# A 32-pair attention kernel with soft mixture of experts: row-tiled score products, block-diagonal queries, one fp32 memory product, padded v, and a new order of all attention operations

## The chip, the cores and the metric

The kernel runs on one core of one Trainium2 chip. The metric is the device time of one execution in microseconds; the time given for a kernel is the median of its runs. The engines named below are PE (matrix products; PEld is its loading of the stationary operand), DVE (vector), ACT (scalar, activations), POOL (GpSimd) and SP, whose queue issues nearly all DMAs.

## The reference

```
scores = scale * q @ k.T, causal mask, softmax over keys        # B 8, H 8, S 576, D 64
local  = a @ v
q_p    = where(q > 0, q, exp(q) - 1) + 1
mem    = (q_p @ M_prev) / (q_p @ z_prev + 1e-6)
x      = g * mem + (1 - g) * local          # g = sigmoid(beta) per head; x: 4608 x 512
# soft mixture of experts on x: 32 slots (8 experts x 4)
logits = x @ phi; dispatch = softmax over tokens; combine = softmax over slots
slot_out = relu((dispatch.T @ x) @ w1) @ w2                     # w1, w2: 33.5 MB
out    = combine @ slot_out
```

All data are fp32. The scores are spread widely enough (q and k are scaled by 8) that they are formed from parts: each operand is split into a high part that the fast one-pass format fp32r holds, and the low rest.

## The kernel before

**Pairs.** The attention goes over 32 pairs of heads, numbered n; a pair's two heads lie on partitions 0-63 and 64-127 of q. A pair's score rows are cut into tiles: `q1h0 ... q3h1` are 128 query rows of one head, with 256, 384 and 512 keys; `a`, `b` and `z` hold 64 query rows of both heads (rows 0-63, 64-127 and 512-575), and `zb` is the last 64 keys of `z`.

**Scores before.** `X` holds q's high part on the head's own 64 rows and the low part on the other head's rows, so a product with contraction over all 128 rows gives (high + low) times k. `K2` and `KL` hold k's high and low part, on both heads' rows; therefore k comes from memory with both heads on all 128 rows. A tile of one head takes two products of 128 rows (L485 with `K2`, L486 with `KL`). `z` takes four such products (L477 to L480) against zeros in `X`; `a`, `b` and `zb` are plain fp32 products of 64x64 tiles (L474), one for each head. The parts are made by `qhi`, `qlo`, `kn`, `kl`, one operation for each head, on the engine that a table `EV` names (helpers: L399 copies on ACT, L402 on DVE, L404 on POOL; subtractions L453 for q, L459 for k).

**The rest of a pair.** DVE adds the mask and takes each row's maximum (`max`, L514), ACT the exponential (`exp`, L522), PE transposes the result in six banks (`t`, L613), ACT or DVE copies these to `at` (`te`), PE multiplies by v (`av` and `memb`, L673) into PSUM. phi(q) (`qmin`, `qexp`, `qphi`) gives the norms (`norm`, L571), which go through DRAM to be spread over rows (`nrw`, `nrr`: DMA rd, then rb) and scale phi(q) (`qn`, L603); the softmax sums go the same way (`rec`, L527 to L529; `rt`, `rte`, `rrw`, `rrr`: DMA rs, then rm). The memory's product `mema` uses a high and low part of M (`mh`, `ml`) and of phi(q) (`qh`, `ql`) in three fp32r products (L666 to L668) and one fp32 product for 64 rows (L669). `mo` and `xe` add up x on DVE.

**Blocks and the end.** Whenever 512 of the 4608 tokens are complete over the four pairs of a batch, this block is taken into the slots' sums (`x1` ... `x5`). After the last pair the experts' two layers run (L1020, L1037), and the outputs are combined and written (L1094, L1096). 46 of 64 weight tiles of 512 KB are loaded by `w` operations before the experts start; 18 are loaded while they run.

**Order.** A string `SEQ` lists every attention operation; each engine issues its instructions in that order, and waits on semaphores for what the others make. PSUM: two slots of two banks for scores (psS), three banks for everything else (psT), one for `av` (psO). `X`, `K2`, `KL`, `at` and v have one buffer each, k and the exponentials two.

Of the kernel before, what the change touches and what calls it, by code (L numbers as in the profile page):

```python
# [46 lines left out]
qhi.0@0 qhi.1@0 qmin@0 qlo.1@0 qlo.0@0 kn.0@0 gate@0 loadm@0 qexp@0 loadq@1 kl.0@0 w@0 kn.1@0 qphi@0 loadm@1 s.zb@0:0
s.a@0 kl.1@0 s.b@0 loadk@1 s.q3h0@0:1 loadq@2 max.a@0 max.b@0 s.q3h1@0 exp.a@0 max.zb@0 loadk@2 mh@0 exp.b@0 norm@0:0
ml@0 max.q3h0@0 loadv@0 s.q2h0@0 neps@0 s.q2h1@0 qmin@1 nmk@0 exp.q3h0@0 max.q3h1@0 qexp@1 max.q2h0@0 s.q1h1@0:1 s.z@0
exp.q3h1@0 max.q2h1@0 w@1 nred@0 exp.q2h1@0 s.q1h0@0 qphi@1 qhi.1@1 nrw@0 exp.q2h0@0 s.b@1:0 max.z@0 qlo.1@1 norm@1:1  # L50
kn.0@1 t.2@0:2 max.q1h0@0 kn.1@1 kl.0@1 s.a@1 t.1@0:0 exp.q1h0@0 max.b@1 te.2@0 qhi.0@1 s.zb@1 kl.1@1 exp.b@1 qlo.0@1
# [5 lines left out]
te.1@1 s.q2h0@2 qn@1 s.q1h0@2:0 loadv@1 te.0@1 s.q1h1@2 s.q2h1@2 rec@1 loadk@4 t.3@1:2 w@4 t.2@1:0 te.3@1 w@5 s.z@2
te.2@1 mo@0 rt@1:2 mema@0:0 rte@1 rrw@1 t.5@1:2 max.q1h0@2 mh@1 xe.0@0 ml@1 te.5@1 max.q2h1@2 t.4@1:1 exp.q1h0@2 xe.1@0
exp.q2h1@2 qh@1 loadm@2 te.4@1 x3.0@0:2 ql@1 qmin@2 x3e.0@0 memb@1:0 max.a@2 av.0@1 max.zb@2 max.z@2 qexp@2 exp.a@2
av.3@1 qphi@2 exp.z@2 av.2@1 max.q2h0@2 loadq@4 av.1@1 max.q1h1@2 exp.q2h0@2 max.b@2 rrr@1 av.6@1 exp.q1h1@2 norm@2:1  # L60
t.5@2:2 exp.b@2 neps@2 s.q3h1@2:0 loadv@2 te.5@2 nmk@2 mema@1:1 max.q3h1@2 kn.1@3 qhi.1@3 nred@2 t.3@2:2 kl.1@3
exp.q3h1@2 loadm@3 s.q3h0@2 qmin@3 nrw@2 te.3@2 s.zb@3:1 mo@1 s.b@3 qlo.1@3 s.a@3 kn.0@3 qhi.0@3 qexp@3 max.zb@3 max.b@3
max.q3h0@2 exp.b@3 qlo.0@3 s.q2h1@3 nrr@2 qphi@3 exp.q3h0@2 s.q3h1@3:0 max.q2h1@3 mh@2 norm@3:2 kl.0@3 rec@2 loadq@5
exp.q2h1@3 xe.0@1 neps@3 max.a@3 nmk@3 rt@2:2 ml@2 exp.a@3 t.1@2:0 nred@3 loadk@5 rte@2 s.q3h0@3 xe.1@1 te.1@2 nrw@3
t.4@2:2 rrw@2 qn@2 t.2@2:0 te.4@2 x3.1@0:1 qh@2 te.2@2 s.q2h0@3 x3e.1@0 memb@2:2 max.q2h0@3 t.0@2:0 max.q3h0@3
exp.q2h0@3 s.q1h0@3:1 s.q1h1@3 nrr@3 ql@2 s.z@3 exp.q3h0@3 max.q3h1@3 te.0@2 mema@2:1 kn.0@4 max.q1h0@3 rrr@2 exp.q3h1@3
max.z@3 kl.0@4 s.b@4:0 s.a@4 qmin@4 av.0@2 qhi.0@4 max.a@4 loadm@4 qexp@4 max.b@4 max.q1h1@3 qlo.0@4 t.2@3:0 qn@3
exp.z@3 av.2@2 qphi@4 exp.q1h1@3 av.1@2 exp.q1h0@3 xe.0@2 s.zb@4 mh@3 exp.a@4 av.3@2 ml@3 rec@3 kn.1@4 norm@4:2 av.6@2
exp.b@4 max.zb@4 neps@4 kl.1@4 s.q3h0@4:1 loadv@3 te.2@3 mo@2 t.4@3:2 qhi.1@4 max.q3h0@4 t.1@3:0 te.4@3 s.q2h0@4 loadk@6
qlo.1@4 te.1@3 exp.q3h0@4 rt@3:2 nmk@4 t.0@3:0 max.q2h0@4 rte@3 rrw@3 nred@4 s.q3h1@4 te.0@3 s.q2h1@4 xe.1@2 exp.q2h0@4  # L70
t.5@3:2 max.q2h1@4 memb@3:0 t.3@3:1 te.5@3 max.q3h1@4 s.z@4:0 exp.q2h1@4 nrw@4 loadq@6 te.3@3 s.q1h1@4 s.q1h0@4 qh@3
qhi.1@5 s.b@5:1 qhi.0@5 av.0@3 max.q1h1@4 kn.1@5 rrr@3 max.q1h0@4 ql@3 exp.q1h1@4 max.z@4 av.1@3 exp.q1h0@4 qlo.1@5
nrr@4 exp.z@4 kl.1@5 av.3@3 t.3@4:2 exp.q3h1@4 mema@3:1 qlo.0@5 kn.0@5 rec@4 s.zb@5 loadm@5 s.a@5 qmin@5 av.2@3 xe.0@3
kl.0@5 max.zb@5 qexp@5 av.6@3 max.a@5 t.1@4:0 max.b@5 loadv@4 mo@3 exp.a@5 s.q3h1@5:0 te.3@4 mh@4 s.q2h1@5 xe.1@3
loadk@7 ml@4 s.q3h0@5 exp.b@5 max.q2h1@5 rt@4:2 x1.0@0:1 rte@4 max.q3h0@5 exp.q2h1@5 rrw@4 te.1@4 x1.1@0 exp.q3h0@5
t.2@4:2 qn@4 t.4@4:0 x1l@0 te.2@4 s.q2h0@5 x1m@0 te.4@4 t.0@4:1 max.q2h0@5 t.5@4:2 x1e@0 qphi@5 memb@4:0 exp.q2h0@5 qh@4
s.q1h0@5:1 s.z@5 te.5@4 loadq@7 te.0@4 rrr@4 ql@4 s.q1h1@5 kn.0@6 qhi.0@6 av.0@4 max.q1h1@5 kn.1@6 max.q1h0@5 exp.q1h1@5
norm@5:2 x1d@0 max.z@5 qlo.0@6 exp.q1h0@5 av.1@4 neps@5 max.q3h1@5 exp.z@5 x2@0:1 nmk@5 mema@4:2 kl.0@6 qhi.1@6
exp.q3h1@5 x2m@0 s.a@6:1 loadm@6 av.3@4 mh@5 max.a@6 ml@5 x2e@0 rec@5 av.2@4 exp.a@6 qmin@6 nred@5 av.6@4 s.zb@6 loadv@5
s.b@6 x2a@0 mo@4 s.q3h0@6:0 nrw@5 rt@5:1 s.q2h0@6 max.q3h0@6 qlo.1@6 qexp@6 rte@5 exp.q3h0@6 xe.1@4 rrw@5 t.2@5:1 qphi@6  # L80
te.2@5 x4.0@0:2 xe.0@4 norm@6:1 x4a.0@0 t.1@5:0 neps@6 x2s@0 nrr@5 x3.3@0:2 te.1@5 x3.2@0:1 x3e.3@0 nmk@6 t.0@5:0 nred@6
loadq@8 x3e.2@0 t.3@5:2 max.q2h0@6 nrw@6 te.0@5 x4.1@0:1 max.zb@6 max.b@6 rrr@5 te.3@5 kl.1@6 t.5@5:0 exp.b@6 x4a.1@0
x5@0:2 exp.q2h0@6 s.q3h1@6 qn@5 loadk@8 t.4@5:1 x5e@0 max.q3h1@6 s.q2h1@6 nrr@6 qh@5 x3.0@1:2 te.4@5 exp.q3h1@6
s.q1h1@6:0 ql@5 s.q1h0@6 s.z@6 te.5@5 x3e.0@1 max.q2h1@6 memb@5:1 av.0@5 kn.0@7 kn.1@7 max.q1h1@6 max.q1h0@6 exp.q1h1@6
qhi.0@7 kl.0@7 av.3@5 exp.q1h0@6 qlo.0@7 av.2@5 max.z@6 exp.q2h1@6 t.3@6:2 qn@6 exp.z@6 qhi.1@7 av.1@5 kl.1@7 qlo.1@7
av.6@5 s.a@7:1 rec@6 loadv@6 s.zb@7 te.3@6 t.1@6:0 mo@5 s.q3h0@7:0 te.1@6 rt@6:2 s.q3h1@7 rte@6 mema@5:0 rrw@6
# [1108 lines left out]
```

## Time and profile before

| | before |
|---|---|
| runs | 549.18, 553.72, 554.17 us; median 553.72 us |
| profiled execution | span 551.3 us from its first to its last instruction; the page gives no time beside the span |
| PE / DVE / ACT / POOL busy | 494.6 / 446.1 / 374.4 / 269.9 us |
| attention, first to last `rec` | 20.5 to 457.3 us: 31 steps of 14.09 us |
| DMA | 104.94 MB, mean 190 GB/s |

Busy is the time in which an engine has an instruction under way. PE's matrix products are pipelined, and the end of each is modelled, so PE's busy time also holds the tails of products. The chain is the path of work and waits that ended last, followed back from the last instruction.

### The profile page before, as it was taken

Reading aid. Unit: us, or ns where it says so; the run is one execution under the profiler, and the core shown is the slowest. Engines: PE = TensorE matmul, PEld = TensorE weight load, DVE = VectorE, ACT = ScalarE, POOL = GpSimd, SP = SyncE. Lnnn points to the kernel's source line nnn. Section 1 sums busy time; section 2 is a strip of 40 time slices with the busy share of each in tenths; the row PEclk is TensorE's granted clock in tenths of the full one; section 3 lists DMA queues with packets and bytes.
Section 4 is the critical chain, followed back from the end, with each engine's and each line's share of the span. In section 5 each row is a group of like instructions: output and inputs, shape, how many; then the busy total and the mean of one; then the engine's idle time right before and its main releaser. Section 6 shows DMA issues by size and latency. Waiting matters only on the chain.

```text
span 551.3 us, 12391 instructions
## 1 busy us (share of the span) xinstructions
PE 494.6 (90%) x4002; PEld 318.8 (58%) x4002; DVE 446.1 (81%) x1422; ACT 374.4 (68%) x1048; POOL 269.9 (49%) x328
## 2 busy tenths in 40 slices
...
GB/s 302 143 277 142 116 139 118 116 254 182 99 241 215 110 181 140 98 276 114 173 116 183 183 152 127 171 105 154 375 139 147 138 101 299 356 260 413 103 335 321
DMA packets 65776, 104.94 MB, mean 190 GB/s; under 512 B 10736, under 2 KB 41008, under 8 KB 65712
## 3 DMA queue, kind: packets, MB, share of 16 engines
...
q8 instruction: 32, 0.52, 0.4%
q14 instruction: 32, 0.26, 0.2%
q10 hardware_dynamic: 288, 0.09, 0.1%
...
## 4 chain that ended last, share of the span: by engine, by line
DVE 32%; PE 32%; DMA 17%; ACT 6%; issue 5%; POOL 2%; SPq 2%; DVEq 0%; ACTq 0%; POOLq 0%
DMA rb<-rd 8%; PE psT L613 6%; DVE q L514 5%; DVE zq L514 4%; PE oa L673 3%; DMA rd<-rq 3%; PE pf L1020 3%; PE psS L485 3%; DVE KL L459 3%; PE pc L1094 2%; PE psS L486 2%; DMA w<-in_w_dram 2%; DVE qp L603 2%; DVE rq L587 2%; DVE rn L583 2%
## 5 line engine op out<-in xcount | busy, mean ns | idle before, releaser
L522 ACT ACTIVATE q<-q,nm 128x512 f32<-128x512 f32 (+2 forms) x160 | 97.9, 613 | 38.7 <-DVE nm L514 36.8
L399 ACT COPY at<-psT 128x512 f32<-128x512 f32 (+1 forms) x230 | 101.2, 484 | 30.7 <-PE psT L613 18.5
L673 PE MATMUL oa<-at,mv 128*64 128x192 f32 (+4 forms) x640 | 103.0, 437 | 0.0
L485 PE MATMUL psS<-K,X 128*128 128x512 f32 (+2 forms) x192 | 77.4, 410 | 16.3 <-DVE nm L514 14.0
L522 ACT ACTIVATE zq<-zq,nm 128x256 f32<-128x256 f32 (+2 forms) x128 | 69.0, 540 | 24.7 <-DVE nm L514 24.0
L453 POOL TENSOR_TENSOR X<-qq,X 64x64 fp32r<-64x64 f32 (+2 forms) x89 | 81.6, 929 | 8.2 <-DVE X L402 2.4
L613 PE MATMUL psT<-cs,q 128*128 128x128 f32 x480 | 78.3, 285 | 6.4 <-DVE xt L716 2.6
L514 DVE CUSTOM_DVE_ANT_0 q<-psS,mv 128x512 f32<-128x512 f32 (+1 forms) x128 | 76.6, 613 | 3.6 <-PE psS L486 2.4
L613 PEld LDWEIGHTS psT<-cs,q 128*128 128x128 f32 x480 | 56.3, 144 | 19.9 <-DVE xt L716 5.6
L486 PE MATMUL psS<-KL,X 128*128 128x512 f32 (+2 forms) x192 | 65.5, 349 | 1.5 <-DVE KL L459 1.0
L673 PEld LDWEIGHTS oa<-at,mv 128*64 128x64 f32 (+1 forms) x640 | 36.9, 135 | 49.4 <-issue 37.0
L404 POOL TENSOR_SCALAR K<-k 128x512 fp32r<-128x512 f32 x28 | 17.9, 640 | 82.1 <-PE psS L479 56.3
L485 PEld LDWEIGHTS psS<-K,X 128*128 128x128 f32 x192 | 37.4, 195 | 26.7 <-DVE nm L514 15.1
L613 PE MATMUL psT<-cs,zq 128*128 128x128 f32 x288 | 49.7, 283 | 1.0 <-ACT at L399 0.7
L558 POOL TENSOR_SCALAR qp<-qq 128x576 f32<-128x576 f32 x24 | 39.7, 1653 | 19.6 <-PE psT L534 9.2
L459 DVE TENSOR_TENSOR KL<-k,K 128x512 fp32r<-128x512 f32 x50 | 46.6, 933 | 0.2
L603 DVE TENSOR_TENSOR qp<-qp,rb 128x576 f32<-128x576 f32 x32 | 27.6, 863 | 20.3 <-DMA rb<-rd 20.3
L404 POOL TENSOR_SCALAR X<-qq 64x384 fp32r<-64x384 f32 (+2 forms) x75 | 34.3, 471 | 17.2 <-issue 6.9
L486 PEld LDWEIGHTS psS<-KL,X 128*128 128x128 f32 x192 | 37.9, 197 | 3.2 <-DVE KL L459 1.6
L613 PEld LDWEIGHTS psT<-cs,zq 128*128 128x128 f32 x288 | 32.2, 141 | 12.6 <-issue 3.4
L660 POOL TENSOR_TENSOR zq<-qp,zq 128x512 fp32r<-128x512 f32 x26 | 34.7, 1336 | 9.1 <-ACT zq L399 7.5
L522 ACT ACTIVATION_READ_ACCUMULATOR q<-q,nm 128x1 f32 x160 | 30.6, 191 | 0.0
...
## 6 DMA issues: line engine op xcount, KB each, us to landing
...
```

The lines of the kernel that those rows point to most:

```text
L399: nc.scalar.copy(o, i)
L404: ENG = dict(a=act, v=dve, p=lambda o, i: nc.gpsimd.tensor_scalar(out=o, in0=i, scalar1=1.0, scalar2=1.0, op0=ALU.mult, op1=ALU.mult))
L453: ALU_ENG[ev(f"qlo.{h}", n)].tensor_tensor(out=x[ROW[1 - h]], in0=i, in1=x[ROW[h]].bitcast(F32), op=ALU.subtract)
L459: ALU_ENG[ev(f"kl.{h}", n)].tensor_tensor(out=KL[:, h, :], in0=st[n]["k"][h][:, 0:512], in1=K2[:, h, :].bitcast(F32), op=ALU.subtract)
L485: nc.tensor.matmul(o, x[:, h, c:c + 128], k2[:, h, 0:N], start=True, stop=False)
L486: nc.tensor.matmul(o, x[:, h, c:c + 128], kl[:, h, 0:N], start=False, stop=True)
L514: nc.vector.tensor_tensor_reduce(out=sm, in0=src, in1=msk, op0=ALU.add, op1=ALU.min, scale=-0.125, scalar=m0, accum_out=acc_o)
L522: nc.scalar.activation(sm, sm, AF.Exp, scale=-1.0, bias=s["nm"][:, J:J + 1], accum_out=s["sum"][:, J:J + 1])
L558: ALU_ENG[ev("qmin", n)].tensor_scalar(out=st[n]["qp"], in0=st[n]["q"], scalar1=0.0, scalar2=None, op0=ALU.min)
L603: nc.vector.tensor_tensor(out=s["qp"], in0=s["qp"], in1=s["rb"], op=ALU.mult)
L613: nc.tensor.transpose(out=ps[:, 128 * x:128 * x + 128], in_=src[:, k0:k0 + 128], identity=ident)
L673: nc.tensor.matmul(o[ROW[h], col:col + nx], vt[rows, c, ROW[h]], st[n]["at"][rows, a0 + hs * h:a0 + hs * h + nx], start=start, stop=stop)
```

## The change

1. **Row-tiled scores** (`op_s`, new L433). `X` holds q's high part in one plane and its low part in the other, each head on its own 64 rows; `K2` the same for k. Three products per head, each over 64 rows, give high x high + low x high + high x low; the two heads' products alternate and write to different PSUM banks, for which `z` moves between `q1h0` and `q1h1`.
2. **Block-diagonal queries** (L427). q comes with 384 more columns: for `a`, `b` and `z` a 128x128 block that holds head 0's 64 rows and head 1's 64 rows on its diagonal. These tiles become one fp32 product over 128 rows for both heads; `z` is cut at a bank's end into two of 256 keys.
3. **One split per pair.** `qhi`, `qlo`, `kn`, `kl` run once per pair on 128 partitions (128x384 for q, 128x512 for k) instead of once per head; k comes once (288 KB instead of 576 KB a pair), q with its blocks (480 KB instead of 288 KB).
4. **The memory in one fp32 pass** (L592): `mh`, `ml`, `qh`, `ql` go; one fp32 product of 512 columns.
5. **Padded v.** v has six chunks, with zeros in the unused halves of the first and last, so that `av` and `memb` always contract over 128 rows; it is loaded in two DMAs.
6. **Smaller edits.** `rec` takes two DVE instructions instead of three; `at` is one fixed tile; 44 instead of 46 weight tiles are loaded before the experts.
7. **New order.** `SEQ`, `EV` and `WORD` (where weight tiles go) are written anew.

```
 def op_s(n, t):
...
-        if t in ("a", "b", "zb"):
-            for h in range(2):
-                r = ROW[h]
-                lo, k0, k1, c = {...}[t]
-                nc.tensor.matmul(ps[r, c:c + k1 - k0], s["q"][r, lo:lo + 64], s["k"][h][r, k0:k1], start=True, stop=True)
-        elif t == "z":
...
-        else:
-            i, h = int(t[1]), int(t[3])
-            c = 128 * (i - 1) + 128 * h
-            o = ps[:, c0:c0 + N]
-            nc.tensor.matmul(o, x[:, h, c:c + 128], k2[:, h, 0:N], start=True, stop=False)
-            nc.tensor.matmul(o, x[:, h, c:c + 128], kl[:, h, 0:N], start=False, stop=True)
+        if t in ("a", "b", "z", "zb"):
+            i, k0, k1, c = {...}[t]
+            cuts = [k0] + [x - c + k0 for x in (512,) if c < x < c + k1 - k0] + [k1]
+            for x0, x1 in zip(cuts, cuts[1:]):
+                nc.tensor.matmul(ps[:, c + x0 - k0:c + x1 - k0], s["qd"][:, i], s["k"][:, x0:x1], start=True, stop=True)
+        else:
+            i = int(t[1])
+            for x, y in ((0, 0), (1, 0), (0, 1)):
+                for h in range(2):
+                    c0, N = WHERE[f"{t}h{h}"][1:3]
+                    nc.tensor.matmul(ps[:, c0:c0 + N], X[ROW[h], x, 128 * i - 128:128 * i], K2[ROW[h], y, 0:N],
+                                     start=(x, y) == (0, 0), stop=(x, y) == (0, 1))
...
-    [("q1h0", 0, 256), ("q1h1", 256, 256), ("z", 512, 576)],
+    [("q1h0", 0, 256), ("z", 256, 576), ("q1h1", 768, 256)],
...
-    def op_kl(n, h):
-        ALU_ENG[ev(f"kl.{h}", n)].tensor_tensor(out=KL[:, h, :], in0=st[n]["k"][h][:, 0:512], in1=K2[:, h, :].bitcast(F32), op=ALU.subtract)
+    def op_kl(n):
+        ALU_ENG[ev("kl", n)].tensor_tensor(out=K2[:, 1, :], in0=st[n]["k"][:, 0:512], in1=K2[:, 0, :].bitcast(F32), op=ALU.subtract)
...
 def op_mema(n):
-        nc.tensor.matmul(om, mh[:, 0], s["qh"], start=True, stop=False)
-        nc.tensor.matmul(om, mh[:, 1], s["qh"], start=False, stop=False)
-        nc.tensor.matmul(om, mh[:, 0], s["ql"], start=False, stop=True)
+        nc.tensor.matmul(om, s["m"][:, 0:128], s["qp"][:, 64:576], start=True, stop=True)
...
 def op_rec(n):
-        nc.vector.tensor_scalar(out=r, in0=st[n]["sum"], scalar1=1e-9, scalar2=None, op0=ALU.add)
+        nc.vector.scalar_tensor_tensor(out=r, in0=st[n]["sum"], scalar=1e-9, in1=omg[:, n % NP, 0:9], op0=ALU.add, op1=ALU.mult)
         nc.vector.reciprocal(out=r, in_=r)
-        nc.vector.tensor_tensor(out=r, in0=r, in1=omg[:, n % NP, 0:9], op=ALU.mult)
```

How this moves instructions is seen in three places. First PE in the middle of the attention, before: the scores of one pair among the transposes (psT) of another. psS is the scores' PSUM, zq and mh are the memory's operands in parts, and the numbered q is a tile that also holds M.

```order
L485 MATMUL psS_2840<-K_104,X 128x384
L486 MATMUL psS_2840<-KL,X 128x384
L474 MATMUL psS_2840<-k,qq 64x128 x2
L485 MATMUL psS_2873<-K_104,X 128x512
L486 MATMUL psS_2873<-KL,X 128x512
L666 MATMUL psT_2916<-zq,mh 128x512
L667 MATMUL psT_2916<-zq,mh 128x512
L668 MATMUL psT_2916<-zq,mh 128x512
L669 MATMUL psT_2843<-qp,q_2506 128x64
L534 MATMUL psT_2922<-cs,r 9x128
```

The same kind of place in the new order (a norm, a block's product, a small tile, an earlier pair's memory product, and the tiles with 512 and 384 keys):

```order
L518 MATMUL psT_3180<-qp,q_3023 32x144 x4
L725 MATMUL psT_3185<-xk,ext 32x256 x4
L427 MATMUL psS_3196<-k,qq 128x64
L592 MATMUL psT_3200<-qp,q_2839 128x512
L593 MATMUL psT_3176<-qp,q_2839 128x64
L433 MATMUL psS_3211<-K_104,X 128x512 x6
L433 MATMUL psS_3196<-K_104,X 128x384 x6
L734 MATMUL psT_3238<-cs,rm 128x128
```

One head's tile was two products, and the tiles of a pair stood apart; now both heads' six products stand together, and a pair's scores take three such places. The memory has one product of 512 columns instead of three.

POOL, before, in a stretch of a little over one pair (X and K are the parts of q and k, zq and mh those of the memory, qp is phi(q)):

```order
L404 TENSOR_SCALAR zq<-qp 128x512
L404 TENSOR_SCALAR X<-qq 64x448
L453 TENSOR_TENSOR X<-qq,X 64x448
L660 TENSOR_TENSOR zq<-qp,zq 128x512
L650 TENSOR_TENSOR mh<-q_2718,mh 128x128
L404 TENSOR_SCALAR X<-qq 64x64
L404 TENSOR_SCALAR X<-qq 64x384
L453 TENSOR_TENSOR X<-qq,X 64x64
L453 TENSOR_TENSOR X<-qq,X 64x384
L558 TENSOR_SCALAR qp<-qq 128x576
```

POOL in the new order, in a stretch of a little over one pair:

```order
L360 TENSOR_SCALAR X<-qq 128x384
L405 TENSOR_TENSOR X<-qq,X 128x384
L360 TENSOR_SCALAR K_104<-k 128x512
L411 TENSOR_TENSOR K_104<-k,K_104 128x512
L505 TENSOR_SCALAR qp<-qq 128x576
```

The subtraction for k's low part has come to POOL (25 of 32 of them; before, 50 of 64 stood on DVE), and everything of the memory's parts is gone. Over the whole program POOL's instructions go from 333 to 143, set-up included.

More of the change, by code (lines that the diff above doesn't have):

```diff
@@ L46 @@
 SEQ = """
[L47 to L51, printed above, removed]
@@ L57 @@
[L57 to L61, printed above, removed]
@@ L62 @@
[L62 to L86, printed above, removed]
@@ new lines @@
+mema@4:21 max.q2h0@5 exp.q2h1@5 qlo@6 exp.q3h0@5 x2@0:0 max.q1h1@5 loadm@6 qmin@6 memb@4 x2a@0 av.0@4 exp.q2h0@5
+loadq@7 max.z@5 max.b@5 av.3@4 exp.z@5 kl@6 av.1@4 max.a@5 exp.a@5 av.6@4 xe.0@4 av.2@4 exp.q1h1@5 x2m@0 exp.b@5
+s.q3@6:1 loadv@5 mo@4 exp.q1h0@5 qexp@6 s.q2@6:0 rec@5 loadk@7 xe.1@4 nrw@5 t.0@5:1 w@2 qphi@6 s.a@6 te.0@5 s.zb@6
+rt@5:0 t.5@5:2 max.q3h0@6 rte@5 nrr@5 t.3@5:1 te.5@5 max.q3h1@6 s.b@6 t.1@5:0 x2e@0 te.3@5 te.1@5 s.q1@6:1 x2s@0
+x4.0@0:2 qhi@7 norm@6:1 max.zb@6 x4a.0@0 x3.2@0:0 neps@6 max.a@6 max.q2h0@6 exp.q3h1@6 t.2@5:2 nmk@6 max.q1h0@6 x5@0:1
@@ new lines @@
+max.q1h0@7 rte@6 max.b@7 kl@8 qexp@7 te.0@6 rrw@6 t.1@6:2 qn@6 s.zb@8:1 te.1@6 t.3@6:0 qlo@8 max.z@7 t.2@6:1 x3.1@1:2
+te.2@6 qphi@7 s.q3@8:0 exp.b@7 rrr@6 te.3@6 exp.q1h0@7 exp.q2h0@7 norm@7:1 max.q3h0@8 av.0@6 w@5 exp.q1h1@7 neps@7
+nmk@7 loadq@9 exp.z@7 nred@7 av.3@6 w@6 av.1@6 max.q3h1@8 exp.a@7 nrw@7 exp.q2h1@7 loadk@9 x3e.1@1 av.6@6 av.2@6
+exp.q3h1@7 memb@6:0 mema@6:1 loadv@7 mo@6 rec@7 s.b@8 xe.1@6 qmin@8 loadm@8 s.a@8 t.2@7:2 nrr@7 exp.q3h1@8 s.q1@8:0
+te.2@7 s.q2@8 max.q1h0@8 xe.0@6 rt@7:1 kn@9 t.5@7:2 max.q2h1@8 rte@7 rrw@7 t.0@7:0 max.zb@8 kl@9 te.5@7 max.b@8
```

583 lines of the change are left out of this document (265 added, 318 removed).

## The prediction

> **What bounds the kernel now.** First the page's head and first part, for the load of each engine over the whole run.
>
> ```profile
> span 551.3 us, 12391 instructions
> ## 1 busy us (share of the span) xinstructions
> PE 494.6 (90%) x4002; PEld 318.8 (58%) x4002; DVE 446.1 (81%) x1422; ACT 374.4 (68%) x1048; POOL 269.9 (49%) x328
> ```
>
> Next the same by stage, in the middle of the attention, from 100 to 400 us (columns: length, then busy time of PE, PEld, DVE, ACT, POOL, granted clock, DMA share, GB/s), and one DVE line that comes once per pair (`rec`, columns: durations, then first and last start).
>
> ```profile
> 100.00:400.00 300.00, 277.23 (x2225) 182.13 (x2223) 260.33 (x866) 228.43 (x660) 192.18 (x233) 0.99 0.57 171
> L528 DVE RECIPROCAL r<-r x32: 215/216/219, 20.5 to 457.3; 128x9 f32<-128x9 f32 x32
> ```
>
> 436.8 us over 31 steps is 14.09 us a pair. Of each 14.09 us PE is busy 13.02 (92.4%), DVE 12.23 (86.8%), ACT 10.73, POOL 9.03; the clock is full (0.99). Attention and its run-in hold 457 of 551 us, so the kernel's time is mostly 31 times this step. Then the page's chain, and the longest waits that bear on it.
>
> ```profile
> DVE 32%; PE 32%; DMA 17%; ACT 6%; issue 5%; POOL 2%; SPq 2%; DVEq 0%; ACTq 0%; POOLq 0%
> POOL K L404 <- PE psS L479: 56.3, 16, 7.6
> ACT q L522 <- DVE nm L514: 36.8, 23, 4.1
> DVE qp L603 <- DMA rb<-rd: 20.3, 12, 3.1
> PE psS L485 <- DVE nm L514: 14.0, 12, 2.5
> ```
>
> The chain is shared by PE and DVE in equal parts. PE waits for DVE's maxima to free score PSUM (14.0 us), ACT for the same maxima (36.8 us), DVE chiefly for a DMA (20.3 us). POOL waits most (56.3 us) for room in `K2`, so POOL's own load isn't the bound. Two engines at 87 and 92% pace the step; a saving counts if it is taken from both.
>
> **The change: PE.** PE's spacing, start to start, tells what a product occupies; its duration holds a tail. From PE's timeline (columns: start us, length us, engine, line, shape):
>
> ```profile
> 258.79 0.47 PE L666 MATMUL psT<-zq,mh 128*128 128x512 f32 x1
> 259.10 0.39 PE L667 MATMUL psT<-zq,mh 128*128 128x512 f32 x1
> 259.32 0.40 PE L668 MATMUL psT<-zq,mh 128*128 128x512 f32 x1
> 259.56 0.33 PE L669 MATMUL psT<-qp,q 128*128 128x64 f32 x2
> ...
> 263.26 0.42 PE L485 MATMUL psS<-K,X 128*128 128x384 f32 x1
> 263.51 0.34 PE L486 MATMUL psS<-KL,X 128*128 128x384 f32 x1
> 263.69 0.28 PE L485 MATMUL psS<-K,X 128*128 128x256 f32 x1
> 263.81 0.28 PE L486 MATMUL psS<-KL,X 128*128 128x256 f32 x1
> ...
> 251.56 0.44 PE L474 MATMUL psS<-k,qq 64*64 64x128 f32 x4
> ```
>
> A one-pass product takes 0.22 us for 512 columns (259.10 to 259.32), 0.18 for 384, 0.12 for 256. The first of a group takes some 0.08 more (0.31 against 0.22, 0.25 against 0.18), since its weights load in view.
> Before, a pair's six head tiles: 4 x (0.22 + 0.18 + 0.12) = 2.08 us, and with up to six group heads 2.56. After, three products for each head: if the two heads run side by side on their halves of the array, 3 x 0.52 + 3 heads = 1.80 us, **0.76 less**; if they run one after the other, 6 x 0.52 + 0.24 = 3.36, **0.80 more**. No row shows two products on different rows and the same columns. The nearest is L474, two heads on 64x64 tiles: a single such product lasts 0.29 us (mean of its 128-column form, quoted below), and four in a row take 0.44, where four in single file, 0.11 apart (the spacing of such an instruction, worked out below), would take 0.62; these run side by side. I take side by side and keep the other end.
>
> The Trainium skill speaks against the full gain. Its page "TensorE: Matmul & The Clock Gate", Part 3, "Measured speedup vs the span model", gives 3.07 times for four row tiles, about 0.77 of the ideal; no run here shows it. As an estimate by that page, two tiles would give 1.54 times, 2.03 us for the products instead of 1.56, and the sum would be 0.47 us a pair worse.
>
> The memory and the small tiles:
>
> ```profile
> L673 PE MATMUL oa<-at,mv 128*64 128x512 f32 x128 | 34.5, 618 | 0.0
> L478 PE MATMUL psS<-KL,X 128*128 128x512 f32 x32 | 12.6, 394 | 0.0
> L474 PE MATMUL psS<-k,qq 64*64 64x128 f32 x128 | 13.7, 290 | 0.6 <-DVE nm L514 0.6
> ```
>
> An fp32 product is recorded as two instructions (128 for 64 products in L673); of 512 columns each lasts 0.618 us against 0.394 one-pass, so each occupies 0.22 + 0.22 = 0.44, and one of 128 columns a quarter of it, 0.11. `mema` goes from 0.31 + 0.22 + 0.24 = 0.77 to 2 x 0.44 + 0.08 = 0.96: 0.19 more. `z` goes from four one-pass products of 512 (0.96) to four instructions of 256 columns at twice 0.11 each (0.88 + 0.08): nothing. `a`, `b`, `zb` become half as many instructions of the same columns that no longer share the array: nothing, bounds 0.2 either way by a group head or two. Padded v has the same columns: nothing, same bounds.
> PE in sum: -0.76 + 0.19 = **-0.57 us a pair** (or +0.99 with heads in single file).
>
> **The change: DVE, ACT, POOL.** Groups with shapes kept apart (count | busy us, mean ns):
>
> ```profile
> L459 DVE TENSOR_TENSOR KL<-k,K 128x512 fp32r<-128x512 f32 x50 | 46.6, 933 | 0.2
> L402 DVE CAST mh<-q 128x128 fp32r<-128x128 f32 x26 | 10.2, 392 | 0.0
> L529 DVE TENSOR_TENSOR r<-r,rm 128x9 f32<-128x9 f32 x32 | 10.3, 321 | 1.1
> L583 DVE TENSOR_TENSOR rn<-rn,rm 128x144 f32<-128x144 f32 x26 | 12.2, 468 | 3.2 <-ACT rn L576 2.9
> L402 DVE COPY at<-psT 128x512 f32<-128x512 f32 x14 | 9.5, 684 | 2.2 <-PE psT L613 1.5 <-PE oa L673 0.4 <-PE psT L862 0.2
> L402 DVE COPY xk<-psT 128x512 f32<-128x512 f32 x4 | 2.7, 687 | 0.5 <-PE psT L794 0.4
> L399 ACT COPY at<-psT 128x512 f32<-128x512 f32 x117 | 67.5, 587 | 25.6 <-PE psT L613 14.0 <-PE oa L673 10.9
> ```
>
> Leaving DVE: 43 of 50 `kl` (40.1 us), 26 casts of M (10.2), one of three `rec` instructions (10.3), 16 of 26 norm masks (7.5). Coming to DVE from ACT by the new table: 19 copies of `at` (13.0) and 8 of `xk` (5.5). Smaller moves on both sides about cancel. Net -49.6 us, **-1.55 us a pair**, to 10.7. ACT loses those 27 copies at its own 0.59 us a piece, some 16 us, and gains 9 `qmin`: about -0.4 a pair. POOL:
>
> ```profile
> L459 POOL TENSOR_TENSOR KL<-k,K 128x512 fp32r<-128x512 f32 x14 | 19.0, 1355 | 3.2 <-issue 2.0 <-ACT K L399 0.5
> L453 POOL TENSOR_TENSOR X<-qq,X 64x384 fp32r<-64x384 f32 x29 | 31.0, 1069 | 0.0
> L404 POOL TENSOR_SCALAR X<-qq 64x384 fp32r<-64x384 f32 x26 | 14.4, 555 | 0.0
> L404 POOL TENSOR_SCALAR K<-k 128x512 fp32r<-128x512 f32 x28 | 17.9, 640 | 82.1 <-PE psS L479 56.3 <-issue 7.3 <-DVE mrun L743 5.8
> L558 POOL TENSOR_SCALAR qp<-qq 128x576 f32<-128x576 f32 x24 | 39.7, 1653 | 19.6 <-PE psT L534 9.2 <-PE psT L669 4.6 <-DVE r L529 2.3
> ```
>
> After, 25 x 1.36 + 26 x 1.07 + 23 x 0.56 + 16 x 0.64 = 84.9 us, and with 19 `qmin` at 1.65 and 22 norm masks at DVE's 0.47 some 127 us in all, half of 269.9. If POOL did a pair's whole splitting in a row it would take 0.64 + 0.56 + 1.07 + 1.36 = 3.6 us, and since `X` and `K2` have one buffer, this stands between a pair's last score product and the next pair's first full group. Behind it PE has transposes, `z`, `av` and `mema` to do, mostly over 4 us; I cost it at nothing. Without that cover it costs up to 3.6 us in a pair.
>
> **DMA and the end.** A pair's k falls by 288 KB and q grows by 192 KB: 3 MB less of 104.94 MB in all. The second DMA for v costs SP one issue a pair: nothing. After the last `rec` come 15 weight loads instead of 11, 2 MB at some 300 GB/s, 7 us if nothing covers them; since the last of them are used only in the experts' second layer, I take 0 and keep 7. The stage after 457.3 us (94 us) and the first 20.5 us I leave as they are.
>
> **The sum.** PE's need falls from 13.02 to 12.45 us a pair, DVE's from 12.23 to 10.7. If PE kept its 92.4%, the step would be 13.47: it gains 19 us. If PE never waited, 12.45: it gains 51. DVE, the engine it waited for, now has slack of 1.8 us a step, so I take the step near the second end, 12.75 us, PE busy at 97.6%: 31 x 1.34 = 41.5 us. The span would be 509.8 us; the median stands 2.4 above the profiled span now, so **512 us**.
>
> **Rivals.**
> *Heads in single file.* If the two heads' products don't overlap, PE's need is 13.02 + 0.99 = 14.01 us, more than the whole DVE load, and at 97.6% the step is 14.35: 31 x 0.26 = 8 us more; at PE's old share 15.2, 33 us more. I price it at **566 us**, slower than before. It decides once less than a sixth of the overlap is had: the step is back at 14.09 when 1.30 of the 1.56 us are lost. For it speaks that no row shows such a pair; against it L474.
> *Half the overlap.* As above with half of 1.56 us lost: 12.45 + 0.78 = 13.23, step 13.55, **537 us**. By the Trainium skill's page named above, 0.47 us would be lost, which as an estimate gives 528.
> *The split chain shows.* `X` and `K2` in one buffer and all of a pair's split in one piece: if 1 us of the 3.6 stands open in each pair, 31 us of the gain go, **543 us**. Against it stand the page's lines of the score products, with the idle time before them and who ended it:
>
> ```profile
> L485 PE MATMUL psS<-K,X 128*128 128x512 f32 (+2 forms) x192 | 77.4, 410 | 16.3 <-DVE nm L514 14.0 <-POOL X L453 1.2 <-DVE X L453 0.6
> L486 PE MATMUL psS<-KL,X 128*128 128x512 f32 (+2 forms) x192 | 65.5, 349 | 1.5 <-DVE KL L459 1.0 <-POOL KL L459 0.5
> ```
>
> PE waits for the parts of q and k 3.3 us in the whole run. But now it waits for one head's parts; then for both.
>
> *DVE paces.* If PE's products overlap better than their spacing and its heads vanish in wider groups, DVE's 10.7 us at its old 86.8% would set 12.3: **498 us**.
>
> **How the numbers follow.** Forecast 0.58 (own range 500 to 528), DVE paces 0.08, half the overlap 0.10, split chain 0.10, single file 0.14. The range goes from 489 (DVE pacing at 89% instead of 86.8%) to 545, past the split chain's case; it leaves out the single file case and a few per cent at the ends. A measurement of this kernel can tell about 1% from no change; faster by over 1% is below 548: the first four cases, less 0.05 for their tails. Single file lies above 559 but for 0.01.
>
> **What would show it.** Right: the spacing of the `rec` reciprocal falls to about 12.75 us; L433's products start in twos, a group of six with 512 columns lasting some 0.85 us (single file: 1.5); DVE busy near 395, POOL near 130, PE busy at least 95% in the attention's middle. Wrong: L433 starts evenly 0.2 us apart; PE or PEld waiting for `X` or `K2` from POOL, ACT or DVE with tens of us; the time from the last `rec` to the end well over 94 us; DVE over 400.

## The result, and the profile after

The changed kernel takes **535.5 us** (median of 4 runs, 531.6 to 541.8) beside 552.2 us before on the same chip; the ratio is 0.969, 95% interval 0.960 to 0.978. The forecast was 512 us: the direction was right, the gain of 17 us is less than half of the 40 forecast. The profiled execution took 531.6 us. Head and first part of its page:

```profile
span 529.8 us, 11904 instructions
## 1 busy us (share of the span) xinstructions
PE 462.5 (87%) x3970; PEld 312.9 (59%) x3970; DVE 384.3 (73%) x1324; ACT 342.4 (65%) x985; POOL 126.0 (24%) x138
```

The same stretch and the same `rec` line as before (length, busy time of PE, PEld, DVE, ACT, POOL, clock, DMA share, GB/s; then durations, first and last start):

```profile
100.00:400.00 300.00, 268.71 (x2276) 185.93 (x2276) 236.43 (x845) 210.50 (x628) 85.14 (x90) 0.98 0.56 160
L476 DVE RECIPROCAL r<-r x32: 215/216/217, 17.0 to 442.3; 128x9 f32<-128x9 f32 x32
```

425.3 us over 31 steps is 13.72 us a pair, against 14.09 before and 12.75 forecast. PE is busy 12.29 of it (89.6%), DVE 10.81 (78.8%), ACT 9.63. So PE got less work than was forecast (12.45) and DVE about as much (10.7), and yet **PE's share fell from 92.4 to 89.6%**, where it was to rise to 97.6%. The span is 21.5 us shorter: 31 x 0.37 = 11.5 from the steps, 6.5 behind the last `rec` (87.5 us instead of 94.0), 3.5 in the run-in.

The chain that ended last, and waits that bear on it (ACT's for PE's transposes, the longest, was 18.5 us before; ACT is busy only 70% of the time):

```profile
PE 36%; DMA 25%; DVE 21%; SPq 6%; ACT 5%; issue 4%; POOL 1%; DVEq 0%; POOLq 0%; ACTq 0%
ACT at L355 <- PE psT L560: 49.1, 55, 3.9
DVE qp L550 <- DMA rb<-rd: 21.2, 15, 2.7
DVE xt L626 <- DMA rm<-rs: 18.1, 10, 4.3
ACT q L470 <- DVE nm L462: 15.2, 13, 3.3
PE psS L427 <- DVE nm L462: 12.0, 18, 1.8
PE psT L518 <- DMA q<-in_M_dram: 7.3, 4, 2.6
PE psS L433 <- DVE nm L462: 6.1, 10, 1.1
```

Two of these, the waits for r's read-back (`rm`) and for M, were hardly there before:

```profile
DVE xt L708 <- DMA rm<-rs: 1.8, 3, 0.8
PE psT L571 <- DMA q<-in_M_dram: 0.7, 1, 0.7
```

DVE's share of the chain fell (32 to 21%), DMA's rose (17 to 25%). The new waits on DMA (16.3 us of DVE for r's read-back, 6.6 of PE for M, some 4 of PE for k and v) come to 27 us; DVE's wait for the norms' read-back (`rb`) was there before (20.3 us); between the forecast step and the real one lie 31 x 0.97 = 30 us. That points at the DMAs, but a sum of waits is not yet a cause.

All kernels that ran, with the ratio to the kernel before and the spacing of `rec` in the profiled execution. Where that execution was over 1.5% longer than the kernel's fastest, no step is given, since it can't be set against the others; the 0.44 us a step that e17's expectation takes from e15 come from such an execution (549.6 us). e1, e2 and e6 to e10 leave something out or compute wrong scores: they measure, and can't replace the kernel.

| run | what differs from the changed kernel | median us | ratio, 95% interval | step us |
|---|---|---|---|---|
| changed kernel | | 535.5 | 0.969 (0.960 to 0.978) | 13.72 |
| e1_trips | round trips not used | 525.1 | 0.955 (0.949 to 0.961) | 13.64 |
| e2_trips_loads | that, and M, v not loaded | 495.1 | 0.898 (0.894 to 0.902) | 12.54 |
| e3_heads_in_file | products in order of heads | 535.9 | 0.969 (0.963 to 0.976) | |
| e4_loads_on_act_queue | q, k, M from ACT's queue | 550.1 | 1.001 (0.995 to 1.006) | 14.05 |
| e5_m_own_buffers | M in three buffers, earlier | 533.6 | 0.960 (0.948 to 0.971) | |
| e6_m_own_v_unread | that, v loaded and not read | 531.5 | 0.956 (0.946 to 0.965) | 13.60 |
| e7_loads_out | M, v not loaded | 512.5 | 0.928 (0.921 to 0.935) | 13.12 |
| e8_heads_same_rows | both heads on rows 0 to 63 | 549.5 | 1.000 (0.997 to 1.003) | 14.18 |
| e9_no_loop_all_bytes | e1 and e6 together | 515.6 | 0.931 (0.919 to 0.944) | 12.97 |
| e10_v_loop_alone | e1 and e5 together | 526.8 | no interval | |
| e11_rec_early | `rec` ahead of the last `mo` | 540.2 | 0.984 (0.975 to 0.993) | 13.80 |
| e12_rec_early_m_own | e11 and e5 together | 536.4 | 0.980 (0.971 to 0.988) | 13.69 |
| e13_issues_merged | four DMAs fewer a pair | 665.5 | 1.212 (1.205 to 1.218) | 17.74 |
| e14_v_one_issue | v in one DMA | 525.2 | 0.944 (0.937 to 0.951) | 13.36 |
| e15_two_issues_more | two small DMAs more | 541.3 | 0.983 (0.979 to 0.987) | |
| e16_loads_on_pool_queue | q, k, M from POOL's queue | 544.4 | 0.989 (0.985 to 0.993) | 14.18 |
| e17_v_qk_one_issue | v in one DMA, q and k in one | 531.9 | 0.966 (0.957 to 0.974) | |
| e18_v_qk_m_own | e17 and e5 together | 530.7 | 0.966 (0.959 to 0.973) | 13.61 |

The fastest complete kernel is e14, 525.2 us, 2.5 points under the changed one with intervals apart.

### The profile page after: what moved, and what is told of

It is laid out like the page before. It is cut to its first block, busy times and chain, and to the rows that moved or that the text cites. A ratio compares the mean times of both kernels' runs of the same rounds, so it can differ in the third digit from the quotient of the medians.

```text
span 529.8 us, 11904 instructions
## 1 busy us (share of the span) xinstructions
PE 462.5 (87%) x3970; PEld 312.9 (59%) x3970; DVE 384.3 (73%) x1324; ACT 342.4 (65%) x985; POOL 126.0 (24%) x138
## 4 chain that ended last, share of the span: by engine, by line
PE 36%; DMA 25%; DVE 21%; SPq 6%; ACT 5%; issue 4%; POOL 1%; DVEq 0%; POOLq 0%; ACTq 0%
PE oa L598 6%; PE psT L560 6%; DMA rb<-rd 5%; PE psS L433 5%; DVE q L462 4%; PE psS L427 4%; DMA rm<-rs 4%; DMA k<-in_k_dram 4%; DMA rd<-rq 3%; DVE zq L462 3%; PE pf L932 3%; DVE qp L550 3%; PE pc L1006 3%; PE psT L592 3%; DMA q<-in_M_dram 2%
## 5 line engine op out<-in xcount | busy, mean ns | idle before, releaser
L355 ACT COPY at<-psT 128x256 f32<-128x256 f32 (+1 forms) x202 | 86.5, 479 | 52.3 <-PE psT L560 49.1
L470 ACT ACTIVATE q<-q,nm 128x512 f32<-128x512 f32 (+2 forms) x160 | 97.6, 612 | 15.3 <-DVE nm L462 15.2
L598 PE MATMUL oa<-at,mv 128*64 128x320 f32 (+4 forms) x640 | 93.1, 427 | 3.0 <-DMA mv<-in_v_dram 1.3
L427 PE MATMUL psS<-k,qq 128*128 128x256 f32 (+2 forms) x320 | 69.2, 330 | 16.5 <-DVE nm L462 12.0
L433 PE MATMUL psS<-K,X 64*128 64x512 f32 (+2 forms) x576 | 70.5, 365 | 8.5 <-DVE nm L462 6.1
L427 PEld LDWEIGHTS psS<-k,qq 128*128 128x128 f32 x320 | 51.9, 199 | 28.3 <-DVE nm L462 17.6
L433 PEld LDWEIGHTS psS<-K,X 64*128 64x128 f32 x576 | 46.1, 188 | 26.9 <-issue 9.8
L598 PEld LDWEIGHTS oa<-at,mv 128*64 128x64 f32 x640 | 38.1, 137 | 38.0 <-issue 27.0
L550 DVE TENSOR_TENSOR qp<-qp,rb 128x576 f32<-128x576 f32 x32 | 27.0, 843 | 21.2 <-DMA rb<-rd 21.2
L626 DVE TENSOR_TENSOR xt<-oa,rm 128x448 f32<-128x448 f32 (+7 forms) x60 | 23.8, 435 | 24.2 <-DMA rm<-rs 18.1
L411 POOL TENSOR_TENSOR K<-k,K 128x512 fp32r<-128x512 f32 x25 | 32.8, 1314 | 31.3 <-ACT K L355 18.9
L358 DVE COPY at<-psT 128x512 f32<-128x512 f32 (+1 forms) x59 | 32.4, 570 | 10.1 <-PE psT L560 8.6
L592 PE MATMUL psT<-qp,q 128*128 128x512 f32 x64 | 35.1, 629 | 4.4 <-DVE qp L550 3.1
```

The costliest lines, as they stand in the source:

```text
L355: nc.scalar.copy(o, i)
L358: nc.vector.tensor_copy(out=o, in_=i)
L411: ALU_ENG[ev("kl", n)].tensor_tensor(out=K2[:, 1, :], in0=st[n]["k"][:, 0:512], in1=K2[:, 0, :].bitcast(F32), op=ALU.subtract)
L427: nc.tensor.matmul(ps[:, c + x0 - k0:c + x1 - k0], s["qd"][:, i], s["k"][:, x0:x1], start=True, stop=True)
L433: nc.tensor.matmul(ps[:, c0:c0 + N], X[ROW[h], x, 128 * i - 128:128 * i], K2[ROW[h], y, 0:N], start=(x, y) == (0, 0), stop=(x, y) == (0, 1))
L470: nc.scalar.activation(sm, sm, AF.Exp, scale=-1.0, bias=s["nm"][:, J:J + 1], accum_out=s["sum"][:, J:J + 1])
```

## The experiments

The edits are shown in short form. The round trips are those through DRAM of the norms (`rd`, then `rb`) and of the softmax sums r (`rs`, then `rm`).

Theory A: data that come late by DMA took the slack of PE and DVE. Theory B, its rival: the new order of the operations, in which PE and DVE hand score PSUM to each other, sets the step, and the waits on DMA fall into idle time.

**Are the waits on DMA the price?**

```diff
-in1=s["rb"]           # qn
+in1=acc[:, 0:288]     # read twice
-in1=rr[:, ...]        # mo, xe
+in1=acc[:, ...]
```

> Leaves out the use of both round trips: `qn`, `mo` and `xe` multiply by a resident tile instead of `rb` and `rr`; the trips' DMAs are still issued. Theory A (DMA that arrives late took the slack: DVE waits 39 us in the whole run for `rb` and `rm`, and PE then waits for DVE): the step falls from 13.72 to 13.0-13.2 us, the span by 15 to 22 us, to some 510. Theory B (the new order itself, PE and DVE handing PSUM to each other, sets the step, and DVE's waits are only idle time of an engine with slack): the span falls by less than 5 us.

```diff
-for h in range(2):                    # op_loadv
+for h in range(2 if n == 0 else 0):
-nc.sync.dma_start(out=m, in_=M[b, p]) # op_loadm
+st[n]["m"] = acc[:, 0:160]
```

> As the kernel without the round trips' use, and v and M are loaded for the first pair alone or not at all (the products read resident data), so that in the middle only the loads of q and k can be late. Theory A: the remaining waits of PE for M and v (8.6 us) go too, and the SP queue is shorter, so k and q come earlier: step 12.7 to 12.9 us, PE busy at 95% or more, span about 500. Theory B: within 10 us of the changed kernel, PE still under 92%.

Without the round trips' use (e1) 10 us went, less than Theory A expected and more than B; PE's waits grew, for M from 7.3 and for v from 1.3 us:

```profile
PE psT L518 <- DMA q<-in_M_dram: 15.1, 7, 6.3
...
PE oa L598 <- DMA mv<-in_v_dram: 6.4, 4, 2.6
```

In e2 no wait of PE or DVE on these transfers is left, and the step is shorter than forecast:

```profile
100.00:400.00 300.00, 286.66 (x2481) 198.43 (x2478) 257.27 (x926) 227.49 (x683) 93.34 (x98) 0.99 0.49 146
L475 DVE RECIPROCAL r<-r x32: 215/216/218, 17.1 to 405.8; 128x9 f32<-128x9 f32 x32
```

PE at 95.6%, 388.7 / 31 = 12.54 us, with the very order of operations that Theory B blames. B fell: the order lets PE run near the 97.6% that the forecast took, once no data come late. (The step comes out below 12.75 because PE is busy 11.98 us of it there, not 12.45.) No run takes these waits out of the kernel before, so how much of the 40 us the old order would have gained too is not known.

**Which of them, and is it the wait or the bytes?** A1 says that M and v wait on SP for their buffers and hold up what stands behind them, A2 that it is their 400 KB a pair.

```diff
+mp = ctx.enter_context(tc.tile_pool(name="mp", bufs=3))
-m = st[n]["m"] = smt(n, "m")
+m = st[n]["m"] = mp.tile([128, 160], F32, name="m")   # loadm a pair earlier in SEQ
```

e5:

> M gets three buffers of its own instead of a piece of the tile `q2`, and each load of M stands in the order where that of the pair before stood, a pair earlier. Theory A1 (what is late is late because loads of M and v wait on SP for their buffer, and hold up what is issued behind them): PE's waits for M (7.3 us) go, SP's waits in front of L396 (some 25 us) too; span 8 to 15 us shorter than 529.8. Theory A2 (it is the bytes: M and v are 400 KB of a pair's DMA): the bytes are the same, so within 5 us.

```diff
-nc.tensor.matmul(o[ROW[h], col:col + nx], vt[:, c, ROW[h]],
+nc.tensor.matmul(o[ROW[h], col:col + nx], acc[:, 64 * c:64 * c + 64],
```

e6, and e7, which leaves these loads out:

> As the kernel with M in buffers of its own; and `av` and `memb` take a resident tile instead of v, whose loads are still issued, with all their bytes, but wait for no product and no product waits for them. A1: as good as leaving the loads out, 500 to 512 us. A2: above 520 us.

> M and v are not loaded in the loop (the products read resident data), the round trips are used as in the changed kernel. With the trips' use also left out it was 495 us. If the trips' waits are a price of their own on top (10 us, as the first run of this kind alone showed): 505. If they were late only because the loads of M and v stood ahead of them on SP: 495 to 500. A1 expects it within 4 us of the kernel whose v is loaded and not read, A2 at least 10 us under that.

A1 fell: with M's buffers its own and v read by nobody, 531.5 us; with both not loaded, 512.5, as A2 expected (the DMAs' bytes and their issues on SP go together here), and 17 us over e2, which doesn't use the round trips either. So the trips have a price of their own. The next kernel, e9, took the waits for M, v and the trips away and left every DMA in place, by joining the edits above; e10 reads v again. Theory C is taken up below:

> All DMAs are issued with all their bytes; M has three buffers of its own, v's loads are issued and not read, and `qn`, `mo`, `xe` multiply by a resident tile. So no engine waits for v, M or a round trip. Theory C (latency, not bytes: the new order puts `mo` of a pair ahead of the next pair's `rec`, so each step contains r's whole round trip, 12.3 us, and 1.7 us from `mo` to the next `rec`; the loop of v's single buffer and of M's is as long): with no loop left the step is 12.5 to 12.8 us as where the loads were left out too (12.54), the median 495 to 503 us. Theory A2 (bytes and issues on SP): the bytes are still there, so 13.2 us or more, 515 us or more.

> As the kernel without loops, but v is read again, in its one buffer: the next load waits on SP for the last `av` of the pair before. What this is slower than the kernel without loops is the price of v's loop: by Theory C, whose second loop was M's and v's together (13.64 us with both), between 12.6 and 13.6 us a step, 500 to 525 us; I take 508.

```profile
100.00:400.00 300.00, 279.99 (x2393) 192.59 (x2390) 246.85 (x896) 218.78 (x656) 92.23 (x96) 0.98 0.57 167
L483 DVE RECIPROCAL r<-r x32: 215/216/218, 17.0 to 419.1; 128x9 f32<-128x9 f32 x32
```

e9's step is 402.1 / 31 = 12.97 us, PE at 93.3%: between the two expectations. So of the 1.18 us that lie between 13.72 and 12.54, 0.75 are waits for the round trips, M and v, and 0.43 go only with the DMAs of M and v themselves. These are steps of single executions, e9's of 507.5 us, beside a median of 515.6. By the ratios (0.969, 0.931, 0.898) the parts are 3.8 and 3.3 points, each uncertain by more than one: **about half are waits, and about half go only with these DMAs**.

e10's four runs lie between 516.9 and 530.0 us, so what v's wait is worth alone is not shown. Taking a part of the waits away brought 0.9 to 1.4 points of the ratio (e1, e5, e6), all together 3.8. That the next late transfer takes the place of the one removed is seen in PE's waits in e1; the ratios alone don't show it, since their intervals allow a plain sum too.

**Is it r's round trip in the order?** From the trace, means over pairs 5 to 28, in us: from `rec` to the end of r's copy, to the write's issue, the write, to the read's issue, the read, from its landing to `mo`, from there to the next `rec`.

```
          rec-copy  issue  write  gap  read  slack to mo  mo to next rec
before    3.09      0.19   3.37   0.91 4.46  3.34         -1.00
after     2.91      1.17   3.07   0.20 4.20  0.73          1.71
```

The trip takes 11.6 us instead of 12.0, but the new order calls for its result 12.3 us after `rec` instead of 15.4, ahead of the next pair's `rec` instead of behind it: 15 of 24 `mo` start within 0.4 us of the landing, before it was 4. Theory C took this loop for the cause and cut it:

```diff
+for n in range(1, 32):      # SEQ, where the last exp of n and xe.0 of n - 1 allow it
+    # rec@n ahead of mo@n-1, rt 5, rte 8, rrw 10 operations behind it
-        ps = st[n]["rt"] = bank()
+        ps = st[n]["rt"] = ob(n - 1)[:, 128:256] if n in EARLY else bank()
```

e11, and e12 with M's own buffers:

> Nothing is left out. In 20 of the 31 steps `rec` stands ahead of the `mo` of the pair before (as soon as the last exponential allows), its transpose 5, its copy 8 and its write 10 operations behind it; the transpose goes to free columns of the bank `ob`. Theory C: it cuts r's loop but not that of M and v, so alone it brings what leaving the trips' use out brought, 0 to 10 us. A2 and B: nothing, within 5 us.

> Nothing is left out: `rec` early in 20 steps, and M in three buffers of its own. Theory C: the loops of r and M are cut in most steps, v's is left: 510 to 525 us, the fastest complete kernel so far. A2 and B: 530 or more.

Waits in e11:

```profile
DVE qp L568 <- DMA rb<-rd: 19.2, 12, 3.7
DVE xt L644 <- DMA rm<-rs: 13.7, 6, 6.6
...
PE psT L536 <- DMA q<-in_M_dram: 9.0, 4, 4.9
```

DVE's wait for r fell from 18.1 to 13.7 us, yet the kernel was no faster (0.984 beside 0.969, the intervals overlap by three thousandths), and e12 took 536.4 us, not 510 to 525. But the edit loosened the loop rather than cut it: over the same pairs the read lands 1.46 us ahead of `mo` instead of 0.73, and 10 of 24 `mo` still start within 0.4 us of the landing. What speaks against r's trip as the single cause is rather e1, which uses neither trip and gains 10 of the 23 us that the forecast was off, and e9, whose 12.97 us lie above the 12.5 to 12.8 that C expected.

**Is it SP's queue?** Theory D: SP issues every DMA of the attention one after the other and stands still until each written r or norm has landed. From the trace's SP rows, a pair: before 13.8 issues, 6.0 us of issuing, 2.3 us of waiting ahead of the read-backs; after 14.8, 7.1 and 3.1. The page's waits of SP ahead of the read-backs, before and after:

```profile
SPq L599 <- DMA rd<-rq: 41.1, 23, 3.7
...
SPq L550 <- DMA rs<-rts: 9.2, 8, 2.3
```

```profile
SPq L546 <- DMA rd<-rq: 54.7, 27, 4.3
SPq L497 <- DMA rs<-rts: 30.9, 29, 2.9
```

And the issues of v, from the tile's own view, before, after, and in one DMA again (ns min, median, max):

```profile
L433 SPq DMA_DIRECT2D mv<-in_v_dram x32: 327/360/602, 10.0 to 461.7; - x32
```

```profile
L391 SPq DMA_DIRECT2D mv<-in_v_dram x64: 470/582/973, 6.1 to 444.6; - x64
```

```profile
L388 SPq DMA_DIRECT2D mv<-in_v_dram x32: 328/422/1542, 5.9 to 432.8; - x32
```

An issue of 64 partitions took longer here than one of 128, and there are two: 2 x 0.58 us for 0.36 before and 0.42 in one DMA again (e14, below).

```diff
-nc.sync.dma_start(out=qq[:, n % 2], in_=q[...])          # and k, M
+nc.scalar.dma_start(out=qq[:, n % 2], in_=q[...])        # e16: nc.gpsimd
```

e4 and e16:

> The loads of q, k and M are issued from ACT's queue, everything else stays on SP's. Theory A in the form that SP's order holds things up (a load waits behind a read-back that waits for its write to land): waits for M and `rm` shrink, the step falls by 0.2 to 0.4 us, the span by 6 to 12 us, less what ACT pays (three issues of 0.35 to 0.5 us a pair, on an engine at 70%). In the form that the transfers themselves are slow (56% of the DMA engines' time is taken), or by Theory B: no change within 5 us, or slower by what ACT pays.

> Nothing is left out; the loads of q, k and M are issued from POOL, which is busy 24% of its time, instead of SP: 1.4 us less of SP's time a pair. Theory D: 515 to 530 us, unless POOL's own queue holds the loads up behind its waits for PE and ACT; then slower than the changed kernel, as it was from ACT's queue (550).

```diff
-for h in range(2):
-    nc.sync.dma_start(out=vt[ROW[h], h:h + 5], in_=v[b, p, ROW[h]])
+nc.sync.dma_start(out=vt, in_=v[b, p])      # v stored with its zeros
```

e14:

> Nothing is left out; only v comes in one DMA with its zeros instead of two of 64 partitions, so 0.6 us less of SP's time a pair, and 64 KB more. Theory D: 3 to 9 us faster than the changed kernel. The prediction's step (the second DMA costs nothing): the same within 3 us.

```diff
+for h in range(2):                          # op_loadk
+    nc.sync.dma_start(out=pad[ROW[h], h], in_=k[b, 128 * p:128 * p + 64, 0:4])
```

e15:

> The dose the other way: two DMAs more a pair on SP, of 1 KB each (64 partitions by 16 bytes, into a tile that nothing reads), 1.1 us of issue, no bytes to speak of, nobody waits for them. Theory D: the step grows by 0.4 to 1.1 us, the median by 12 to 35 us. If SP's issue time is hidden: the same within 4 us.

```diff
+nc.sync.dma_start(out=rr, in_=st[n]["rs"]...broadcast_to([2, 64, S]))   # r's read-back in one
+nc.sync.dma_start(out=rd[:, 128:512], in_=rts[0:6])                     # two writes in one
+nc.sync.dma_start(out=qq[:, n % 2], in_=q[...])                         # k lies behind q; v as above
```

e13, then e17 and e18, which leave r's trip as it was:

> Nothing is left out; four DMAs fewer a pair: q and k come in one, v with its zeros in one (64 KB more), the read-back of r in one instead of two, its write in three instead of four. Theory D (SP's queue is the engine that runs out: of a step of 13.72 us it spends 7.1 us on issuing 14.8 DMAs and 3.1 us waiting for the writes of the round trips to land, against 6.0 and 2.3 us before the change, so whatever DMA is next comes late): 1.9 us less of issue a pair, the step 13.0 to 13.4 us, 510 to 527 us. If the bytes are what counts, or latency alone: within 4 us of the changed kernel (535.5).

> Nothing is left out: v in one DMA, q and k in one, everything else as in the changed kernel, r's round trip untouched. So far a DMA less on SP gave 0.36 us a step for 0.64 us of issue, and two more cost 0.44 for 1.42. Theory D: 1.1 us of issue less, a step of 13.1 to 13.4 us, 512 to 525 us, the fastest complete kernel. If the 10 us of the single issue for v were v's alone: 525 again. Against it: k now lands with q, in 768 KB, later than alone.

> As the kernel with v in one and q and k in one issue, and M in three buffers of its own, a pair earlier. Theory D with the waits for M (7 us where v came in one issue): 5 to 10 us less than that kernel. By what M's own buffers brought alone (nothing): the same within 4 us.

One issue for v (e14) gives 10 us and a step of 13.36, although it moves 64 KB more. Its `rec` line, and DVE's waits for the two read-backs:

```profile
L473 DVE RECIPROCAL r<-r x32: 215/216/218, 16.7 to 430.7; 128x9 f32<-128x9 f32 x32
DVE xt L623 <- DMA rm<-rs: 21.6, 13, 4.7
DVE qp L547 <- DMA rb<-rd: 12.2, 11, 2.1
```

v itself landed no sooner: 4.1 us after its issue, where the two DMAs took 4.3 from the first issue to the last landing (medians from 100 to 400 us, from the semaphores' times, as are the landings below). But q and k landed 4.4 and 3.8 us after theirs instead of 4.8 and 4.5, and DVE's wait for the norms' read-back fell from 21.2 to 12.2 us.

Two issues more (e15) cost 6 us, half of the least expected. For 1.4 us of issue a pair this is far less than 10 us for 0.64, so SP's issue time alone does not account for what the second DMA of v costs. With q and k in one as well (e17) the gain is gone, 531.9 us, and M's own buffers add nothing to that (e18, 530.7). e18 has 12.6 issues and 5.8 us of issuing a pair; its q and k land 5.5 us after their issue where alone they took 4.4 and 3.8 in e14, and their joint load stands where the later of the two stood. Loads from another engine's queue (e4, e16) cost 9 to 15 us, although SP's issuing fell to 5.7 and 5.8 us a pair: r's read-back landed 4.0 and 3.7 us after its issue instead of 3.2, and DVE waited longer for it, in e4 and in e16:

```profile
DVE xt L626 <- DMA rm<-rs: 31.0, 15, 5.2
```

```profile
DVE xt L626 <- DMA rm<-rs: 33.7, 13, 6.1
```

e13 does not test D: its merged read-back became slow in itself (last section). **The second DMA of v costs 10 us; Theory D as the whole cause is not borne out**: fewer issues with a later k, or on another queue, were worth nothing.

**Are the row tiles worth what was forecast?**

```diff
-for x, y in ((0, 0), (1, 0), (0, 1)):
-    for h in range(2):
+for h in range(2):
+    for x, y in ((0, 0), (1, 0), (0, 1)):
```

e3:

> The six products of a group in the order of heads: three of the first head, then three of the second, so that only one round of the five can overlap. If the row tiles do run side by side, PE gets two rounds more a group, 2 x (0.24 + 0.18 + 0.12) = 1.08 us a pair, 33 us in all where PE sets the step; by Theory A, PE is idle 1.4 us a pair while it waits for others, so a part is absorbed and the span grows by 10 to 25 us; by Theory B by 25 to 33 us. If the starts 4 ns apart were only how the trace shows them, nothing changes.

```diff
-nc.tensor.matmul(ps[...], X[ROW[h], x, ...], K2[ROW[h], y, 0:N], ...)
+nc.tensor.matmul(ps[...], X[ROW[0], x, ...], K2[ROW[0], y, 0:N], ...)
```

e8:

> Both heads' q products take rows 0 to 63 of the array (the second head's scores are then the first's), so that they cannot overlap. PE needs 3 x (0.24 + 0.18 + 0.12) = 1.6 us more a pair, 50 us in all. Where PE's own work sets the step, the span grows by 45 to 50 us; by Theory A PE has 1.4 us a pair in which it waits, and the span grows by 10 to 35 us. If the changed order of heads cost nothing because rows don't overlap anyway: 0.

A group of six products with 512 columns on PE's timeline (start, length), of the changed kernel, in order of heads, and on the same rows:

```profile
252.73 0.98 PE L433 MATMUL psS<-K,X 64*128 64x512 f32 x6
```

```profile
261.26 0.97 PE L433 MATMUL psS<-K,X 64*128 64x512 f32 x6
```

```profile
265.20 1.66 PE L433 MATMUL psS<-K,X 64*128 64x512 f32 x6
```

On the same rows a group takes 0.68 us more for three rounds more, 0.23 each, a whole product of 512 columns; the overlap is full. Expected of e3 was that only one round of five overlaps; the group is as short as ever, and e3's time, 535.9 us, is the changed kernel's, so the heads overlap in either order. The kernel on the same rows is back at the time before the change, with PE again the bound:

```profile
100.00:400.00 300.00, 286.13 (x2197) 206.50 (x2197) 233.99 (x826) 204.76 (x610) 84.20 (x87) 1.00 0.54 157
```

PE needs 0.954 x 14.18 = 13.52 us there, 1.23 more than 12.29, and the step grew by only 0.46: time in which PE had waited took up the rest, as Theory A expected. So the overlap of the heads is worth 14 us of this kernel's time.

## Why the forecast was wrong, step by step

- **PE's need, -0.57 us a pair to 12.45**: right, 12.29. The memory's product takes 0.96 us to the next start instead of 0.77 (medians), as forecast, and the groups of a pair are 1.55 us shorter than on the same rows (e8, medians), where the sum had 1.56. The side-by-side choice was right and the rival of a single file did not come. By the estimate from the Trainium skill's page "TensorE: Matmul & The Clock Gate", Part 3, "Measured speedup vs the span model", which has a figure for four row tiles, two would lose 0.47 us a pair; the runs show no such loss for two tiles of 64 rows (0.23 us a round in twos and in single file).
- **A group of six in 0.85 us**: 0.98 in the row above. No working for the 0.85 is given, so what it left out is not known.
- **DVE 10.7 us, POOL 127 us in all, ACT -0.4**: 10.81, 126.0, and ACT -1.10 (what took the rest from ACT was not looked for); DVE in all 384 where "near 395" stood.
- **The split chain costs nothing**: right; for `X` and `K2` PE waits 2.1 us and its weight loads 4.6 in the whole run, not tens.
- **The end and the run-in unchanged**: 10 us better together. What shortened them was not tried.
- **"DVE, the engine it waited for, now has slack, so I take the step near the second end", PE at 97.6%**: **the step that failed.** PE's share was 89.6%. Shown for this place: with the waits for the round trips, M and v taken away PE comes to 93.3%, with M's and v's loads gone too to 95.6%, and the steps to 12.97 and 12.54: data that came late by DMA held PE, which the sum had no term for. The slack was real, but the view read for it (who waits for whom now) says nothing of who is next. The trace before held two candidates, r's trip with 3.3 us to spare and SP with 8.3 us of each 14.1 taken; neither is shown to be the whole.
- **"The second DMA for v costs SP one issue a pair: nothing"**: wrong, and a part of the same step. It costs 0.36 us a step, 31 x 0.36 = 11 us, by e14 (525.2 beside 535.5); by what means is open, since e15 prices SP's issue time far lower. The Trainium skill's page "DMA: Bandwidth & Descriptors", "Rules for kernel authors", advises one transfer of 128 partitions over two of disjoint halves; e14 agrees, with 10 us.
- **The range** held the time (489 to 545), at the value of "half the overlap" and by another mechanism, which none of the rivals named. It held by luck in part: without the 10 us that the end and the run-in gave unforeseen, the time would have been some 545, at the range's edge.

Open: what makes the transfers late. The half that goes only with M's and v's DMAs may be SP's time or the transfers'; e14 and e15 show that an issue more or less counts, e4, e16, e17 and e18 that it is not the whole.
